# Logits of four units in one set of matmuls, the groups' work in small pieces between scans, and zeros written from SyncE's queue

## The chip, the cores and the metric

The kernel runs on one core of one Trainium2 chip. The time is the device time of one launch in microseconds (us); the time of the kernel before is the median of three runs.

## What is computed

The input is a batch of 4 sequences of 5056 tokens with 256 features (20224 tokens in all, fp32). A gated recurrence runs along each sequence; its output goes to a router that picks one of 8 experts for each token; each expert keeps the 80 tokens it weighs highest and runs a two-layer network on them. All other tokens get zeros.

```python
sig = 1.0 / (1.0 + np.exp(-f_logit))
f = lower_bound + (1.0 - lower_bound) * sig
for t in range(S):                       # S = 5056, for 4 sequences and 256 features
    h = f[:, t] * h + (1.0 - f[:, t]) * x[:, t]
    y[:, t] = h
logits = y.reshape(20224, 256) @ w_gate  # 8 experts
expert_idx = np.argmax(logits, axis=1)
gate_w = softmax(logits)[arange, expert_idx]
out = np.zeros((20224, 256))
for e in range(8):
    tok_idx = the 80 tokens of expert e with the largest gate_w
    h = np.maximum(x[tok_idx] @ w1[e], 0.0)          # 256 x 1024
    out[tok_idx] = gate_w[tok_idx, None] * (h @ w2[e])
```

## The kernel before, in words

**First stage.** The work is cut into 40 units of 512 tokens: 10 groups, each with one unit of each of the 4 sequences. A unit goes through SP (`load`: its tiles `f_t` and `x_t`, 512 KB each, 4 buffers each), ACT (`gate`: the sigmoid, in place), POOL (`enter`: the product, in place), PE (`to_channels`: 8 transposes of `f_t` into the PSUM tiles `sp`, 8 of `x_t` into `up`, so that features are on the partitions), ACT (`decay`: writes the factors into the unit's place in `h_all`) and DVE (`scan`: the recurrence, two scans of 512 steps, one for each half `o` of the features, in place in `h_all` with `up` as second operand). `h_all` is one large SBUF tile with the states of all 20224 tokens.

**The groups' work.** `logits` multiplies a unit's states with the router's weights on PE. The four interleaved token positions `r` go to four strips of 32 output partitions, so the moving operand is read with a step of 4 elements (16 bytes). The result of a group is the PSUM tile `lg`; ACT copies it to `ls`; PE transposes it back to tokens, `lt`; DVE finds the largest logit and its expert (`mx`, `shift`, `eq`, `pick`). After groups 3, 6, 8 and 9 a batch of further steps follows (exponentials on ACT, `sums`, `gated` with DVE and POOL, `turned` on PE, `candidates`, `peaks`), one job in each round of the main loop. The round `n` writes, in this order: load n+3, gate n+2, enter n+2, transposes n+1, decay n+1, scan n, logits n-1, then a group's `by_token` and `choice`, then one job. The order of instructions on each engine is the order in which the code writes them; an engine that waits holds up all that stands behind it.

**Selection.** From the largest candidates of each partition DVE and PE rank the tokens of all experts; `trow` holds the chosen token numbers. This is a single chain (lines 419 to 492).

**Experts.** For each expert the 80 states are copied out of `h_all` by DVE (28), ACT (28) and POOL (24), each of which first loads its token numbers from `trow` into its registers (line 515); `scaled` makes `xt`; then `hidden` (PE, `h_ps`), `relu` (ACT), `result` (PE, `y_ps`), `finish` (DVE) and `scatter` (POOL, rows of the output). The weights come over SP's queue into a ring of 7 tiles of 512 KB. All output rows are first written with zeros: 20 transfers of about 1 MB, which ACT issues before its first `gather`:

```python
    w_sb = {}
    for key in order[:3]:
        w_sb[key] = weights(*key)
    for k in clears:
        clear(nc.scalar, k)
```

PSUM has 8 banks: `sp` 2, `up` 3, `lg`, `lt` and `ct` (the turned candidates) 1 each.

Of the kernel before, what the change touches and what calls it, by code (L numbers as in the profile page):

```python
# [22 lines left out]
def kernel(  # L23
# [128 lines left out]
    with tc.tile_pool(name="ld", bufs=4) as ld, \  # L152
         tc.tile_pool(name="gsm", bufs=1) as gsm, \
         tc.tile_pool(name="pss", bufs=2, space=PSUM) as pss, \
         tc.tile_pool(name="psu", bufs=3, space=PSUM) as psu, \
         tc.tile_pool(name="plg", bufs=1, space=PSUM) as plg:

        xs, fs, sts, uts, sps, ups, lgs, lts, shs, gts, gms, cts = ({} for _ in range(12))
# [6 lines left out]
        def setup():  # L165
# [7 lines left out]
            bp = plg.tile([P, 1], F32, name="bp", tag="lt")  # L173
# [59 lines left out]
        def logits(n):  # L233
            g, b = divmod(n, B)
            if b == 0:
                lgs[g] = plg.tile([P, B, P], F32, name="lg", tag="lg")
            hv = h_all[:, :, ds(spot(n), G)].rearrange("c o (p r) -> c o p r", r=R)
            for o in range(DC):
                for r in range(R):
                    nc.tensor.matmul(lgs[g][ds(r * LC, LC), b], wg[:, o], hv[:, o, :, r],  # L240
                                     start=o == 0, stop=o == DC - 1, skip_group_check=True)

        def by_token(g):
            ls = gsm.tile([P, B, P], F32, name="ls", tag="ls")
            nc.scalar.copy(ls, lgs.pop(g))  # L245
            lt = plg.tile([P, B, P], F32, name="lt", tag="lt")
# [11 lines left out]
        def choice(g):  # L258
# [23 lines left out]
        def sums(g0, g1):  # L282
            n = g1 - g0
            sm = gsm.tile([P, per_batch, C], F32, name="sm", tag="sm")[:, ds(0, n)]
            nc.vector.tensor_reduce(sm, shs.pop(g0)[:, ds(0, n)], AX.X, ALU.add)
# [4 lines left out]
        def gated(g):  # L290
# [397 lines left out]
```

## Time and profile before

| | |
|---|---|
| median of three runs | 302.87 us (302.01 to 303.67) |
| the profiled execution, its own time | 303.26 us |
| its span in the trace | 301.4 us |
| busy in the span: PE, DVE, POOL, ACT | 207.6, 180.6, 135.2, 133.3 us |
| bytes read and written | 58.73 MB and 21.36 MB |
| mean granted TensorE clock | 0.848 of full speed |

A trace tells of one execution. Busy shares are averages over the three stages, which have different limits; what a stage waits for is read in the stage itself. In rows of the timeline, the two numbers at the front are the start and the length of a run of equal instructions in us, and in brackets stands the idle time of the engine ahead of it and what ended it. "x16" counts records: an fp32 matmul is two records, a transpose one.

### The profile page before, as it was taken

Reading aid. Unit: us, or ns where it says so; the run is one execution under the profiler, and the core shown is the slowest. Engines: PE = TensorE matmul, PEld = TensorE weight load, DVE = VectorE, ACT = ScalarE, POOL = GpSimd, SP = SyncE. Lnnn points to the kernel's source line nnn. Section 1 sums busy time; section 2 is a strip of 40 time slices with the busy share of each in tenths; the row PEclk is TensorE's granted clock in tenths of the full one; section 3 lists DMA queues with packets and bytes.
Section 4 is the critical chain, followed back from the end, with each engine's and each line's share of the span. In section 5 each row is a group of like instructions: output and inputs, shape, how many; then the busy total and the mean of one; then the engine's idle time right before and its main releaser. Section 6 shows DMA issues by size and latency. Waiting matters only on the chain.

```text
span 301.4 us, 5943 instructions
## 1 busy us (share of the span) xinstructions
PE 207.6 (69%) x1756; PEld 162.6 (54%) x1756; DVE 180.6 (60%) x484; ACT 133.3 (44%) x380; POOL 135.2 (45%) x269
## 2 busy tenths in 40 slices
PE   1798596979978896979797420610003999999991
PEld 1676375757655575657575100600003988888870
DVE  1996685858497969679596579314002715665500
ACT  3676456573796564786665100000005454555110
POOL 3876837465646784638581101003403405555111
PEclk9999899797999998998999955575555559999998
DMA  7999979596979896887920999999994448999900
GB/s 211 349 348 350 341 233 324 198 313 198 290 226 299 249 346 198 242 263 220 318 79 0 335 372 409 409 406 388 384 383 157 142 139 265 312 310 305 327 27 27
DMA packets 66439, 80.55 MB, mean 267 GB/s; under 512 B 2784, under 2 KB 52064, under 8 KB 66400
## 3 DMA queue, kind: packets, MB, share of 16 engines
q1 hardware_dynamic: 55040, 58.73, 61.4%
q10 hardware_dynamic: 10976, 20.72, 18.2%
q0 software_dynamic: 384, 0.66, 0.7%
q8 instruction: 16, 0.26, 0.4%
q14 instruction: 23, 0.19, 0.2%
HBM read 58.73 MB, written 21.36 MB: 266 GB/s over the span
## 4 chain that ended last, share of the span: by engine, by line
PE 56%; DVE 17%; issue 14%; ACT 5%; DMA 5%; POOL 1%; SPq 0%; POOLq 0%; DVEq 0%; ACTq 0%
PE lg L240 12%; PE h_ps L537 12%; PE y_ps L552 10%; PE sp L215 9%; PE up L215 8%; DVE h_all L228 6%; ACT h_all L222 3%; DVE eq L271 3%; DMA f_t<-in_f_logit_dram 3%; DVE beat L449 3%; PE lt L248 2%; DMA x_t<-in_x_dram 2%; ACT ls L245 2%; PE flat_p L472 1%; DVE mx L268 1%
## 5 line engine op out<-in xcount | busy, mean ns | idle before, releaser
L209 POOL TENSOR_TENSOR x_t<-f_t,x_t 128x1024 f32<-128x1024 f32 x40 | 94.9, 2375 | 50.2 <-ACT f_t L205 33.6
L228 DVE TENSOR_TENSOR_SCAN h_all<-h_all,up 128x512 f32<-128x512 f32 x80 | 96.2, 1253 | 6.2 <-PE up L215 5.2
L222 ACT ACTIVATE h_all<-sp,nomlb 128x512 f32<-128x512 f32 x80 | 51.1, 684 | 50.4 <-PE sp L215 50.3
L215 PE MATMUL up<-ident,x_t 128*128 128x128 f32 x320 | 48.3, 293 | 22.2 <-DVE h_all L228 20.3
L537 PE MATMUL h_ps<-xt,w_sb 128*128 128x80 f32 x256 | 36.4, 311 | 33.5 <-issue 33.5
L537 PEld LDWEIGHTS h_ps<-xt,w_sb 128*128 128x128 f32 x256 | 36.1, 227 | 34.3 <-issue 33.8
L215 PEld LDWEIGHTS up<-ident,x_t 128*128 128x128 f32 x320 | 40.1, 153 | 25.5 <-issue 20.9
L519 ACT COPY xe<-h_all 128x2 f32 x224 | 22.2, 190 | 67.3 <-DMA out_dram<-zero 56.0
L215 PE MATMUL sp<-ident,f_t 128*128 128x128 f32 x320 | 48.2, 299 | 3.4 <-ACT f_t L205 3.4
L240 PE MATMUL lg<-h_all,wg 128*32 128x128 f32 x640 | 43.9, 404 | 5.4 <-ACT ls L245 4.8
L215 PEld LDWEIGHTS sp<-ident,f_t 128*128 128x128 f32 x320 | 39.7, 154 | 13.4 <-ACT f_t L205 7.0
L205 ACT ACTIVATE f_t<-f_t 128x1024 f32<-128x1024 f32 x40 | 42.4, 1059 | 8.8 <-DMA f_t<-in_f_logit_dram 8.8
L519 POOL COPY xe<-h_all 128x2 f32 x192 | 24.5, 202 | 39.2 <-DVE xt L526 18.5
L519 DVE COPY xe<-h_all 128x2 f32 x224 | 26.5, 180 | 19.6 <-issue 19.6
L552 PE MATMUL y_ps<-w_sb,hid 128*80 128x256 f32 x128 | 30.1, 391 | 0.0
L240 PEld LDWEIGHTS lg<-h_all,wg 128*32 128x32 f32 x640 | 18.3, 120 | 19.2 <-ACT ls L245 7.0
L552 PEld LDWEIGHTS y_ps<-w_sb,hid 128*80 128x80 f32 x128 | 19.4, 156 | 8.1 <-issue 1.0
L561 POOL DMA_INDIRECT out_dram<-y,goal x8 | 7.5, 940 | 34.9 <-DVE y L558 32.5
L268 DVE TENSOR_REDUCE mx<-lt 128x16 f32<-128x128 f32 (+1 forms) x10 | 2.9, 291 | 28.0 <-PE lt L248 28.0
L526 DVE TENSOR_SCALAR xt<-xe,omlb 128x80 f32<-128x80 f32 x16 | 3.5, 258 | 23.6 <-ACT xe L519 22.8
L545 ACT ACTIVATE hid<-h_ps 128x320 f32<-128x320 f32 x16 | 7.0, 436 | 20.8 <-PE h_ps L537 20.8
L558 DVE TENSOR_SCALAR y<-y_ps,gsl 80x256 f32<-80x256 f32 x8 | 3.8, 480 | 20.4 <-PE y_ps L552 20.4
(96 smaller groups left out, 107.2 us busy)
## 6 DMA issues: line engine op xcount, KB each, us to landing
f_t<-in_f_logit_dram SPq DMA_DIRECT2D x40, 512.0 KB, 4.7
x_t<-in_x_dram SPq DMA_DIRECT2D x40, 512.0 KB, 5.3
out_dram<-zero ACTq DMA_DIRECT2D x19, 1024.0 KB, 13.1
w_sb<-in_moe_w_dram SPq DMA_DIRECT2D x32, 512.0 KB, 4.7
out_dram<-zero ACTq DMA_DIRECT2D x1, 768.0 KB, 12.2
out_dram<-y,goal POOLq DMA_INDIRECT x8, 4.0
lb<-in_lower_bound_dram ACTq DMA_DIRECT2D x1, 1.0 KB, 4.1
wg<-in_moe_w_gate_dram ACTq DMA_DIRECT2D x1, 8.0 KB, 5.3
```

The costliest lines, as they stand in the source:

```text
L205: nc.scalar.activation(sts[n], sts[n], ACT.Sigmoid, scale=-1.0)
L209: nc.gpsimd.tensor_tensor(uts[n], sts[n], uts[n], ALU.mult)
L215: nc.tensor.transpose(ps[:, ds(r * P, P)], src[n][:, r, ds(o * P, P)], ident)
L222: nc.scalar.activation(h_all[:, o, ds(spot(n), G)], sps.pop((n, o)), ACT.Identity, scale=nomlb[:, ds(o, 1)], bias=1.0)
L228: nc.vector.tensor_tensor_scan(h, h, ups.pop((n, o)), h_all[:, o, ds(spot(n) - 1, 1)] if n >= B else 0.0, ALU.mult, ALU.add)
L240: nc.tensor.matmul(lgs[g][ds(r * LC, LC), b], wg[:, o], hv[:, o, :, r], start=o == 0, stop=o == DC - 1, skip_group_check=True)
L271: nc.vector.scalar_tensor_tensor(out=eq, in0=sh, scalar=0.0, in1=revexp[:n_p].unsqueeze(1).broadcast_to(full), op0=ALU.is_ge, op1=ALU.mult)
L449: nc.vector.tensor_scalar(beat, rivals, vals[:, ds(k, 1)], 0.0, ALU.is_gt, ALU.add, accum_out=rank[:, ds(k, 1)])
L519: copy(X[e][:, :, ds(k + j, 1)], h_all[:, :, ds(v, 1)])
L537: nc.tensor.matmul(h_ps[:, c], halves[i][:, o, ds(c * P, P)], xt[:, o], start=o == 0, stop=o == DC - 1, skip_group_check=True)
L552: nc.tensor.matmul(y_ps, hid[:, c], halves[c // CH][:, c % CH], start=c == 0, stop=c == FC - 1)
L561: nc.gpsimd.indirect_dma_start(out=out, out_offset=bass.IndirectOffsetOnAxis(ap=goal[:, ds(e, 1)], axis=0), in_=Y.pop(e), in_offset=None, ...
```

## The change

- `logits` takes a whole group at once: 8 matmuls with 512 moving columns instead of 32 with 128, written one round after the group's last scan was written; the copy to `ls` follows it directly in the code.
- The work of a group is three jobs, one in each round after the scan: `logits`; `by_token` with `mx` and `shift`; `eq` with `pick`. Of the batch's jobs, `sums` is cut in two. In the last two rounds two batch jobs run instead of one, and all that is left runs behind the loop.
- `lt` shares the bank of `lg`; `up` has 4 buffers instead of 3.
- The product `gm` of the last three groups is made by DVE instead of POOL.
- The zeros are issued by SP: 14 behind the first six weight tiles, the other 6 in the first expert's round, behind the weights of its successors.

```diff
-         tc.tile_pool(name="psu", bufs=3, space=PSUM) as psu, \
+         tc.tile_pool(name="psu", bufs=4, space=PSUM) as psu, \
...
-        def logits(n):
-            g, b = divmod(n, B)
-            if b == 0:
-                lgs[g] = plg.tile([P, B, P], F32, name="lg", tag="lg")
-            hv = h_all[:, :, ds(spot(n), G)].rearrange("c o (p r) -> c o p r", r=R)
+        def logits(g):
+            lg = plg.tile([P, B * P], F32, name="lg", tag="lg")
             for o in range(DC):
+                hv = h_all[:, o].rearrange("c (b s) -> c b s", b=B)[:, :, ds(first(g), G)]
+                hv = hv.rearrange("c b (p r) -> c b p r", r=R)
                 for r in range(R):
-                    nc.tensor.matmul(lgs[g][ds(r * LC, LC), b], wg[:, o], hv[:, o, :, r],
+                    nc.tensor.matmul(lg[ds(r * LC, LC)], wg[:, o], hv[:, :, :, r],
                                      start=o == 0, stop=o == DC - 1, skip_group_check=True)
+            lss[g] = gsm.tile([P, B, P], F32, name="ls", tag="ls")
+            nc.scalar.copy(lss[g].rearrange("p b t -> p (b t)"), lg)
...
-            nc.gpsimd.tensor_tensor(
+
+            (nc.gpsimd if g < n_grp - 3 else nc.vector).tensor_tensor(
...
-        n = -AHEAD
-        while n < n_unit + 3 or todo:
+        for n in range(-AHEAD, n_unit):
             unit(load, n + AHEAD)
...
             unit(scan, n)
-            unit(logits, n - 1)
-            group(by_token, n - 2)
-            group(choice, n - 2)
-            for job in todo[:1]:
-                for f in job:
-                    f()
-            del todo[:1]
-            group(lambda g: todo.extend(work(*batches[g])) if g in batches else None, n - 2)
-            n += 1
+            some_of(of_group, 1)
+            some_of(of_batch, 1 if n < n_unit - 2 else 2)
+            if n >= 0 and n % B == B - 1:
+                g = n // B
+                of_group += [[lambda g=g: logits(g)], [lambda g=g: shifted(g)],
+                             [lambda g=g: chosen(g)]]
...
-    for k in clears:
-        clear(nc.scalar, k)
+    zeros = list(clears)
+
+    def clear_some(m):
+        for k in zeros[:m]:
+            clear(nc.sync, k)
+        del zeros[:m]
+
+    clear_some(14)
...
                     more(1)
+                if e == 0 and not again:
+                    clear_some(len(zeros))
                 y_ps = result(e)
```

PE, at the end of a group in the kernel before (`sp` and `up` are transposes, `lg` the logits, `lt` the transposes back; in brackets the engines whose progress an instruction waits for):

```order
L215 MATMUL up<-ident,x_t 128x128 [waits DVE_49]
L215 MATMUL up<-ident,x_t 128x128 x3
L240 MATMUL lg<-h_all,wg 32x128 [waits PE_49,Activation_49]
L240 MATMUL lg<-h_all,wg 32x128 x7
L248 MATMUL lt<-ident,ls 128x128 x4
L215 MATMUL sp<-ident,f_t 128x128 [waits PE_49]
L215 MATMUL sp<-ident,f_t 128x128 x3
L215 MATMUL sp<-ident,f_t 128x128 [waits PE_49]
L215 MATMUL sp<-ident,f_t 128x128 x3
L215 MATMUL up<-ident,x_t 128x128 [waits DVE_49,Pool_49]
```

The same place on PE in the changed kernel:

```order
L239 MATMUL lg<-h_all,wg 32x512 [waits DVE_49,Activation_49]
L239 MATMUL lg<-h_all,wg 32x512 x3
L239 MATMUL lg<-h_all,wg 32x512 [waits DVE_49,Activation_49]
L239 MATMUL lg<-h_all,wg 32x512 x3
L215 MATMUL sp<-ident,f_t 128x128 [waits PE_49]
L215 MATMUL sp<-ident,f_t 128x128 x3
L215 MATMUL sp<-ident,f_t 128x128 [waits PE_49]
L215 MATMUL sp<-ident,f_t 128x128 x3
L215 MATMUL up<-ident,x_t 128x128 [waits Pool_49]
L215 MATMUL up<-ident,x_t 128x128 x7
L248 MATMUL lt<-ident,ls 128x128 [waits Activation_49]
L248 MATMUL lt<-ident,ls 128x128 x3
```

The transposes back stand a whole unit's transposes behind the logits now, and each half of the logits waits for DVE and for ACT.

DVE, in the first groups of the kernel before (the scans have the tile `h_all` as output):

```order
L228 SCALAR_TENSOR_TENSOR h_all<-h_all,up 128x512 [waits PE_49,Activation_49] x6
L268 TENSOR_REDUCE mx<-lt 128x16 [waits PE_49]
L269 TENSOR_TENSOR shift<-lt,mx 128x128 [waits DVE_49]
L271 SCALAR_TENSOR_TENSOR eq<-shift,revexp 128x128 [waits DVE_49]
L274 TENSOR_REDUCE pick<-eq 128x16 [waits DVE_49]
L228 SCALAR_TENSOR_TENSOR h_all<-h_all,up 128x512 [waits Activation_49] x2
```

The same place on DVE in the changed kernel:

```order
L228 SCALAR_TENSOR_TENSOR h_all<-h_all,up 128x512 [waits PE_49,Activation_49] x6
L269 TENSOR_REDUCE mx<-lt 128x16 [waits PE_49]
L270 TENSOR_TENSOR shift<-lt,mx 128x128 [waits DVE_49]
L228 SCALAR_TENSOR_TENSOR h_all<-h_all,up 128x512 [waits Activation_49] x2
L278 SCALAR_TENSOR_TENSOR eq<-shift,revexp 128x128 [waits DVE_49]
L281 TENSOR_REDUCE pick<-eq 128x16 [waits DVE_49]
```

The four steps that stood together are cut in two by the scans of one unit.

ACT's instructions at the end of the first stage of the kernel before (`shift` is the last exponential, `trow` the load of token numbers into registers, `xe` the first of 28 copies):

```order
L280 ACTIVATE shift<-shift 128x128
L147 DMA out_dram<-zero 128x4x512 x19
L147 DMA out_dram<-zero 128x3x512
L515 TENSOR_LOAD trow
L519 ISA
L519 COPY xe<-h_all 128x2
```

All 20 issues stand between the last exponential and the first register load; in the changed kernel ACT has none of them. SP's queue in the changed kernel, behind the last loads (`w_sb` are the weight tiles):

```order
L408 DMA w_sb<-in_moe_w_dram 128x2x512 x4
L412 DMA w_sb<-in_moe_w_dram 128x4x256 x2
L147 DMA out_dram<-zero 128x4x512 x14
L408 DMA w_sb<-in_moe_w_dram 128x2x512 x2
L412 DMA w_sb<-in_moe_w_dram 128x4x256 x2
L147 DMA out_dram<-zero 128x4x512 x5
L147 DMA out_dram<-zero 128x3x512
L408 DMA w_sb<-in_moe_w_dram 128x2x512 x2
```

On SP the zeros stand in two runs, 14 and 6, each ahead of weight tiles.

## Rows read from the trace of the kernel before

**Rows 1.** Busy time by stage; then TensorE clock, DMA share, GB/s.

```profile
core 0: us, PE busy (x) PEld busy (x) DVE busy (x) ACT busy (x) POOL busy (x), PEclk, DMA share, GB/s
22.70:167.70 145.00, 119.05 (x1207) 88.35 (x1205) 111.16 (x132) 89.97 (x122) 85.36 (x43) 0.94 0.79 247
167.70:196.70 29.00, 8.95 (x53) 6.52 (x53) 18.74 (x69) 0.90 (x2) 2.95 (x9) 0.59 1.04 389
196.70:230.70 34.00, 0.25 (x2) 0.18 (x2) 4.86 (x41) 2.74 (x28) 6.11 (x48) 0.54 0.99 371
```

**Rows 2.** The chain that ended last, from selection to experts.

```profile
196.48 0.23 DVE trow L474
...
197.14 33.52 issue
230.66 7.09 PE h_ps L537 x32
...
237.87 7.04 PE h_ps L537 x32
244.91 4.68 PE y_ps L552 x16
...
253.12 3.46 PE y_ps L552 x16
```

**Rows 3.** Timeline of ACT from the last logits to its first expert copies.

```profile
168.54 0.59 ACT L245 COPY ls<-lg 128x512 f32<-128x512 f32 x1 [3.99 <-PE lg L240]
...
171.22 49.03 ACTq L147 DMA_DIRECT2D out_dram<-zero  x20
227.46 2.74 ACT L519 COPY xe<-h_all 128x2 f32 x28 [55.96 <-DMA out_dram<-zero]
```

**Rows 4.** Timeline of DVE: the copies of the first and the fourth expert.

```profile
205.82 2.80 DVE L519 COPY xe<-h_all 128x2 f32 x24 [0.26 <-issue]
...
251.68 3.26 DVE L519 COPY xe<-h_all 128x2 f32 x28 [1.57 <-issue]
```

**Rows 5.** DVE by line, 13 to 168 us: busy, mean ns; idle before, releasers.

```profile
L228 DVE TENSOR_TENSOR_SCAN h_all<-h_all,up 128x512 f32<-128x512 f32 x80 | 96.2, 1253 | 6.2 <-PE up L215 5.2 <-ACT h_all L222 1.0
L271 DVE SCALAR_TENSOR_TENSOR eq<-shift,revexp 128x128 f32<-128x128 f32 (+1 forms) x9 | 8.5, 939 | 0.4
...
L268 DVE TENSOR_REDUCE mx<-lt 128x16 f32<-128x128 f32 (+1 forms) x9 | 2.6, 291 | 26.9 <-PE lt L248 26.9
```

**Rows 6.** Timeline of ACT: two sigmoids that waited for their loads.

```profile
17.43 1.06 ACT L205 ACTIVATE f_t<-f_t 128x1024 f32<-128x1024 f32 x1 [0.32 <-DMA f_t<-in_f_logit_dram]
...
20.45 1.06 ACT L205 ACTIVATE f_t<-f_t 128x1024 f32<-128x1024 f32 x1 [0.30 <-DMA f_t<-in_f_logit_dram]
```

**Rows 7.** Timeline of DVE behind the last scan.

```profile
167.64 0.40 DVE L285 TENSOR_REDUCE sm<-shift 128x32 f32<-128x256 f32 x1
...
177.05 0.26 DVE L419 MAX8 vals<-tops 128x8 f32<-128x96 f32 x1
```

**Rows 8.** The zeros' transfers (KB, us to landing), and SP's first weight tiles.

```profile
out_dram<-zero ACTq DMA_DIRECT2D x19, 1024.0 KB, 13.1
...
164.81 1.90 SPq L386 DMA_DIRECT2D w_sb<-in_moe_w_dram  x4
```

**Rows 9.** The register loads (line 515): shortest, median and longest in ns.

```profile
L515 DVEq TENSOR_LOAD <-trow x8: 1849/1858/7112, 197.7 to 277.6; - x8
```

**Rows 10.** Timeline of PE at full clock.

```profile
85.62 1.10 PE L240 MATMUL lg<-h_all,wg 128*32 128x128 f32 x16
86.66 1.09 PE L215 MATMUL sp<-ident,f_t 128*128 128x128 f32 x8
87.58 1.04 PE L215 MATMUL up<-ident,x_t 128*128 128x128 f32 x8
```

**Rows 11.** Timeline of PE at half clock, and the clock of that stretch.

```profile
52.95 1.12 PE L240 MATMUL lg<-h_all,wg 128*32 128x128 f32 x16
54.00 1.97 PE L215 MATMUL sp<-ident,f_t 128*128 128x128 f32 x8
...
52.80:56.00 3.20, 3.20 (x28) 2.55 (x27) 2.87 (x3) 0.69 (x1) 1.17 (x1) 0.50 0.46 156
```

More of the change, by code (lines that the diff above doesn't have):

```diff
@@ L154 @@
          tc.tile_pool(name="pss", bufs=2, space=PSUM) as pss, \
-         tc.tile_pool(name="psu", bufs=3, space=PSUM) as psu, \
+         tc.tile_pool(name="psu", bufs=4, space=PSUM) as psu, \
          tc.tile_pool(name="plg", bufs=1, space=PSUM) as plg:
-        xs, fs, sts, uts, sps, ups, lgs, lts, shs, gts, gms, cts = ({} for _ in range(12))
+        xs, fs, sts, uts, sps, ups, lss, lts, shs, gts, gms, cts, sms = ({} for _ in range(13))
         def spot(n):
@@ L172, in setup @@
                            channel_multiplier=0, allow_small_or_imprecise_dtypes=True)
-            bp = plg.tile([P, 1], F32, name="bp", tag="lt")
+            bp = plg.tile([P, 1], F32, name="bp", tag="lg")
             nc.tensor.transpose(bp, base_row, ident[:1, :1])
@@ L230, in scan @@
                     h_all[:, o, ds(spot(n) - 1, 1)] if n >= B else 0.0, ALU.mult, ALU.add)
-        def logits(n):
-            g, b = divmod(n, B)
-            if b == 0:
-                lgs[g] = plg.tile([P, B, P], F32, name="lg", tag="lg")
-            hv = h_all[:, :, ds(spot(n), G)].rearrange("c o (p r) -> c o p r", r=R)
+        def logits(g):
+            lg = plg.tile([P, B * P], F32, name="lg", tag="lg")
             for o in range(DC):
+                hv = h_all[:, o].rearrange("c (b s) -> c b s", b=B)[:, :, ds(first(g), G)]
+                hv = hv.rearrange("c b (p r) -> c b p r", r=R)
                 for r in range(R):
-                    nc.tensor.matmul(lgs[g][ds(r * LC, LC), b], wg[:, o], hv[:, o, :, r],
+                    nc.tensor.matmul(lg[ds(r * LC, LC)], wg[:, o], hv[:, :, :, r],
                                      start=o == 0, stop=o == DC - 1, skip_group_check=True)
+            lss[g] = gsm.tile([P, B, P], F32, name="ls", tag="ls")
+            nc.scalar.copy(lss[g].rearrange("p b t -> p (b t)"), lg)
         def by_token(g):
-            ls = gsm.tile([P, B, P], F32, name="ls", tag="ls")
-            nc.scalar.copy(ls, lgs.pop(g))
-            lt = plg.tile([P, B, P], F32, name="lt", tag="lt")
+            ls = lss.pop(g)
+            lt = plg.tile([P, B, P], F32, name="lt", tag="lg")
             for b in range(B):
@@ L255, in begin, with shifted @@
             return batch_of(g)[0]
-        def choice(g):
+        def shifted(g):
+            by_token(g)
             n_p = rows(g)
@@ L269, in choice @@
             nc.vector.tensor_tensor(sh, lg, mx.unsqueeze(2).broadcast_to(full), ALU.subtract)
+        def choice(g):
+            n_p = rows(g)
+            full = [n_p, C, E]
+            sh = shs[begin(g)][:n_p, g - begin(g)]
             eq = gsm.tile([P, C, E], F32, name="eq", tag="eq")[:n_p]
@@ L283, in sums, with inverses @@
             n = g1 - g0
-            sm = gsm.tile([P, per_batch, C], F32, name="sm", tag="sm")[:, ds(0, n)]
-            nc.vector.tensor_reduce(sm, shs.pop(g0)[:, ds(0, n)], AX.X, ALU.add)
+            sms[g0] = gsm.tile([P, per_batch, C], F32, name="sm", tag="sm")
+            nc.vector.tensor_reduce(sms[g0][:, ds(0, n)], shs.pop(g0)[:, ds(0, n)], AX.X, ALU.add)
+        def inverses(g0, g1):
+            n = g1 - g0
+            sm = sms.pop(g0)[:, ds(0, n)]
             nc.vector.tensor_scalar_add(sm, sm, 1e-9)
@@ L322, in work @@
         def work(g0, g1):
-            jobs = [[lambda: exponentials(g0, g1)], [lambda: sums(g0, g1)]]
+            jobs = [[lambda: exponentials(g0, g1)], [lambda: sums(g0, g1)],
+                    [lambda: inverses(g0, g1)]]
             for g in range(g0, g1 + 1):
@@ L335, in unit, with chosen, some_of @@
                 f(m)
-        def group(f, m):
-            if 0 <= m < n_unit and m % B == B - 1:
-                f(m // B)
         AHEAD = 3
-        todo = []
+        of_group, of_batch = [], []
+        def chosen(g):
+            choice(g)
+            if g in batches:
+                of_batch.extend(work(*batches[g]))
+        def some_of(jobs, k):
+            while jobs and k:
+                for f in jobs.pop(0):
+                    f()
+                k -= 1
         setup()
-        n = -AHEAD
-        while n < n_unit + 3 or todo:
+        for n in range(-AHEAD, n_unit):
             unit(load, n + AHEAD)
```

4 lines of the change are left out of this document (added).

## The prediction

> **What bounds the kernel now.** I read the stages first [rows 1]. In the first stage (to 167.7 us) no engine is full: DVE is busy 111 of 145 us, PE 119, and DMA moves 247 GB/s. Selection (to 196.7) and the wait behind it (to 230.7) have DMA at 371 to 389 GB/s, its share at 1.0: there the zeros set what DMA does. From 196.7 to 230.7 no engine computes for long.
>
> The chain of waits says what that last stretch is [rows 2]: the chosen tokens (`trow`) are ready at 196.71, and the first expert's matmuls start at 230.66, 33.9 us later. ACT explains it [rows 3]: its 20 zero issues begin at 171.22 and hold its queue for 49.0 us, so that its 28 copies for the first expert run from 227.46 to 230.20. DVE had its own copies done at 205.82 + 2.80 = 208.62 [rows 4]. So ACT's queue alone is late, by 21.6 us.
>
> In the first stage the view by line shows what DVE, the busiest engine in order, waits for [rows 5]: 26.9 us for `lt` (nine times, 3.0 us each) and 6.2 us ahead of scans. DMA isn't the limit there: where sigmoids wait for loads they follow each other by 3.02 us [rows 6], 12.1 us for a group, and a group takes some 16 (144.9 us from the fifth unit's scan at about 22.7 to the last scan's end at 167.64 [rows 1, 7], for nine groups).
>
> **The change part by part.**
>
> *Zeros off ACT.* ACT can load its token numbers when `trow` is there. DMA stays full at that time: six weight tiles (3.1 MB) and 14 zero transfers (14.7 MB) take 46 us at 389 GB/s [rows 1], from about 4 us ahead of the last scan's end (SP issues the tiles when the last `up` is done, now at 164.81 [rows 8]). `trow` comes some 28 us behind that end. A register load took 7.1 us under the zeros and 1.85 us otherwise [rows 9]. I keep 7.1: the first matmul then starts at 208.62 + 0.46 (what now lies between ACT's last copy and it) = 209.1 where it stood at 230.66. **-21.6 us.** With a fast load it would be 5.3 more, with ACT's load starting late up to 2 less.
>
> *The logits of four units.* Sixteen records of 128 columns take 1.04 us to the next stage's start, at 0.23 for four strips that run together [rows 10]. At half clock the same sixteen take as long, 1.12 against 1.10, while eight transposes go from 1.09 to 1.97 [rows 10, 11]. So the clock doesn't set the strips' pace. A contiguous transpose of 128 columns takes 0.115 (eight in 0.92), half of 0.23: I take the read with its step of 16 bytes as the limit, which grows with the columns. Four strips of 512 columns then cost 0.9 us, a half of the features 1.8, a group 3.6 (four times 1.04 now). Bounds: 1.8 us a group if long strips run at the contiguous pace, 7.4 if all sixteen records run one after the other.
>
> By the Trainium skill, SBUF — State Buffer, section "Door 1: The DMA port swizzle", accesses hit full bandwidth when at least two fall in one 16-byte line. A step of four fp32 values puts one in each, which agrees with the factor of two above. The skill's TensorEngine Tiling (Array Packing), section "Tiling Modes", says that tiles run independently, which by itself would give the 1.8 us; the first of the rivals is that case.
>
> *What the logits hold up.* They read all four sequences' places in `h_all` at once. The reordered rows of PE show that this read is taken as the whole stretch between: each half of `lg` waits for DVE and ACT anew, and the `up` behind it no longer waits for DVE. So it waits for the scan of the unit after the group (u0) and the decay of the next (u1), and u1's scans wait for it. With u0's first scan starting at 0 and 1.2 us for a scan [rows 5]: first half of `lg` 1.25 to 3.25 (with 0.2 of drain), u1's first scan at 3.3 where it could at 2.4; second half to 5.05, u1's second scan at 5.1 where it could at 4.5. **DVE waits 1.45 us in each of nine groups, +13.** Behind `lg` stand 16 transposes (0.9 us for eight [rows 10]), to 6.75, and then `lt`, to 7.4; `ls` (0.59 [rows 3]) fits beside them. DVE ends u1's scans at 6.3 and waits 1.1 us for `lt`: **nine times, +10, where it was 26.9.** `eq`, delayed to 0.94 us by POOL's work, stays [rows 5]. Of the scans' own 6.2 us I take off 2.5, since PE stands still for shorter and falls less to half clock (bounds 0 and 6.2). Sum of the first stage: -26.9 + 13 + 10 - 2.5 = **-6.5 us**. The fourth `up` buffer and the shared bank of `lt` cost nothing in this: `lt` needs `ls`, which empties the bank; were that cover gone, the next logits would wait, but they come 8 us later.
>
> *The tail.* From the last scan to `vals` it is 9.4 us now [rows 7]. The leftovers of groups 7 and 8 run under the last logits and DVE makes `gm` without POOL; the last half of logits is 1.1 us longer. I take 8.0, **-1.4** (bounds -2.5 and +1).
>
> *The six late zeros.* SP reaches them when the first half of the second expert's `h_ps` has freed its tile, 10.7 us behind the first matmul [rows 2]. They are 6.0 MB, 15.5 us at 389 GB/s, to 26. The first `y_ps` ends at 18.9 (244.91 + 4.68 - 230.66). DVE then loads the numbers of the fourth expert; now its copies end at 254.94 [rows 4], and the matmuls that need them start at 256.58 (253.12 + 3.46 [rows 2]). With 0.5 for `xt` that leaves 1.1 us, and a load of 7.1 instead of 1.85 takes 5.25: PE stands for 4.2 us. The weights of that expert, behind the zeros in the queue, come at about 28 where 25.9 would do, inside the same stall. The next expert's load meets the weights' backlog, 1.8 more: **+6 us** (bounds 0 and 10, the latter with a fall to half clock).
>
> Sum: -21.6 - 6.5 - 1.4 + 6 = -23.5. The profiled execution took 303.26, so 279.8; it lies 0.4 above the median of the runs, which makes 279.4. **I predict 280 us.**
>
> **The rivals.**
>
> *Long strips run at the contiguous pace* (1.8 us a group). Then u1's scans hardly wait: first half done at 2.4, second at 3.5. Nine times 1.5 us less, about 266. For it speaks that the four start together; against it the same pace at both clocks. Chance 0.16.
>
> *The second stall is worse, or groups stay near 15.5 us*, because the exponentials hold ACT and with it the decay that `lg` now waits for: 288 to 297. For it speaks that each group's pieces now wait on each other in order; against it ACT's 90 busy us in 145 [rows 1]. Chance 0.10.
>
> *Slower than before: the sixteen long records run one after the other*, 7.4 us a group. u1's second scan moves by the whole difference: 3.8 us nine times, 34, which gives 314. It decides from 6.2 us a group on (3.6 + 23.5 / 9). Against it: sixteen records of 128 columns in 1.04 us is less than the 1.84 of a single file. Chance 0.03.
>
> *No gain*: the zeros' issue holds SP as it held ACT, and the tile that SP then has to bring is wanted at once. For it speaks that three of its weight tiles stand behind 14 zeros; against it that the first six tiles stand ahead, and are enough to 18.9 us behind the first matmul. 302, chance 0.01.
>
> **How the numbers follow.** My forecast has 0.70 (272 to 288, by the bounds of its terms). 264 to 291 holds it, the contiguous case and about half of the worse one, over 0.8. No change within 0.5% (what a measurement here can tell) 0.01, slower 0.03, faster 0.96.
>
> **What the profile after would show.** ACT's idle time ahead of its first `xe` without `zero` as releaser, and the first `h_ps` about 12.4 us behind `trow`. DVE's wait for `lt` near 10 us in all; scans that wait for `lg`, about 13 us. Sixteen `lg` records in about 3.8 us. The last scan's end near 161. Long register loads in the first and the fourth expert, and an idle PE of some 4 us ahead of the fourth `h_ps`. Wrong I would be if four strips of 512 columns took far from 0.9 us, or if the register loads were slow for another reason than the zeros.

## The result, and the profile after

The changed kernel takes 292.67 us (median of four runs, 291.17 to 293.64) where the kernel before, run beside it, took 303.27: a ratio of 0.9652 (95% interval 0.96 to 0.9705). The forecast was 280, with a range of 264 to 291. The sign was right; the time lies 1.7 us above the range and 12.7 above the forecast.

The profiled execution took 292.59 us, with a span of 290.8 us, 10.6 shorter than before. The stages first, cut at the last scan's end, at `trow` and at the first expert's matmul (columns as in [rows 1]):

```profile
22.70:165.30 142.60, 114.78 (x758) 71.58 (x756) 116.79 (x134) 87.41 (x122) 84.94 (x43) 0.95 0.80 254
165.30:193.40 28.10, 10.65 (x58) 6.61 (x53) 19.96 (x72) 0.90 (x2) 1.70 (x6) 0.62 1.03 388
193.40:205.70 12.30, 0.21 (x1) 0.11 (x1) 4.73 (x40) 2.74 (x28) 3.02 (x24) 0.64 1.05 399
```

The wait behind `trow` is 12.3 us long where it was 34. But the first stage is only 2.4 us shorter (its last scan ends at 165.3, before at 167.7), and DVE works longer in it: 116.8 us against 111.2 [rows 1]. What comes behind the wait is on PE's timeline:

```profile
205.74 7.09 PE L565 MATMUL h_ps<-xt,w_sb 128*128 128x80 f32 x32 [11.96 <-issue]
...
214.10 7.12 PE L565 MATMUL h_ps<-xt,w_sb 128*128 128x80 f32 x32 [1.15 <-DVE xt L554]
221.01 5.13 PE L580 MATMUL y_ps<-w_sb,hid 128*80 128x256 f32 x16
225.98 3.69 PE L565 MATMUL h_ps<-xt,w_sb 128*128 128x80 f32 x32
229.51 3.62 PE L580 MATMUL y_ps<-w_sb,hid 128*80 128x256 f32 x16
240.91 7.09 PE L565 MATMUL h_ps<-xt,w_sb 128*128 128x80 f32 x32 [7.78 <-DMA w_sb<-in_moe_w_dram]
```

The fourth expert's `h_ps` starts after 7.78 us of idle PE, waiting for weights, and then takes 7.09 us where the third took 3.69. The same place in the chain of waits, and SP's queue (a row is the start of the first issue and the time until the last is through):

```profile
228.15 12.63 DMA w_sb<-in_moe_w_dram
240.91 7.09 PE h_ps L565 x32
248.00 5.18 PE y_ps L580 x16
253.18 3.53 PE h_ps L565 x32
```

```profile
212.86 5.34 SPq L412 DMA_DIRECT2D w_sb<-in_moe_w_dram  x2
218.25 9.80 SPq L147 DMA_DIRECT2D out_dram<-zero  x6
228.15 3.10 SPq L408 DMA_DIRECT2D w_sb<-in_moe_w_dram  x2
```

The weights were issued as soon as the six zeros were through SP, and still took 12.63 us to land; a tile of weights takes 5.2 in the median. Three stretches of this time (the columns again as in [rows 1]) show a full DMA, an idle PE, and the clock behind it:

```profile
220.00:232.00 12.00, 12.00 (x66) 9.54 (x66) 0.51 (x2) 3.83 (x31) 1.06 (x9) 0.83 1.05 398
234.00:238.00 4.00, 0.00 (x0) 0.00 (x0) 3.30 (x25) 0.35 (x3) 0.00 (x0) 0.96 0.96 291
242.00:250.00 8.00, 8.00 (x35) 7.15 (x35) 1.42 (x11) 0.88 (x3) 4.12 (x26) 0.50 0.97 325
```

PE stands still to 240.9 and then runs at 0.50, that is at 1.2 GHz, to 250 at least. The copies of the fourth expert on DVE's timeline:

```profile
233.01 3.26 DVE L547 COPY xe<-h_all 128x2 f32 x28 [6.35 <-issue]
236.41 0.43 DVE L554 TENSOR_SCALAR xt<-xe,omlb 128x80 f32<-128x80 f32 x2
```

DVE waited 6.35 us there for its register load (before 1.57, [rows 4]): with the weights in time PE would have stood from 233.1 to 236.8.

In the first stage, DVE by line (13 to 168 us, as [rows 5]) has the new waits as forecast, 12.4 us for `lg` and 8.9 for `lt`:

```profile
L228 DVE TENSOR_TENSOR_SCAN h_all<-h_all,up 128x512 f32<-128x512 f32 x80 | 97.6, 1258 | 14.3 <-PE lg L239 12.4 <-issue 1.0 <-ACT h_all L222 0.8
...
L269 DVE TENSOR_REDUCE mx<-lt 128x16 f32<-128x128 f32 (+1 forms) x9 | 2.6, 291 | 8.9 <-PE lt L248 8.9
```

But some of its small steps are long: `eq` takes 1.04 us in the mean, 0.94 before [rows 5]. A single one shows why. DVE's and POOL's timelines at 75 to 88 us:

```profile
75.52 2.44 DVE L228 TENSOR_TENSOR_SCAN h_all<-h_all,up 128x512 f32<-128x512 f32 x2
77.88 1.31 DVE L278 SCALAR_TENSOR_TENSOR eq<-shift,revexp 128x128 f32<-128x128 f32 x1
79.23 0.29 DVE L281 TENSOR_REDUCE pick<-eq 128x16 f32<-128x128 f32 x1
...
85.21 1.82 DVE L297 TENSOR_SCALAR sm<-sm 128x64 f32<-128x64 f32 x1
```

```profile
74.36 4.68 POOL L209 TENSOR_TENSOR x_t<-f_t,x_t 128x1024 f32<-128x1024 f32 x2 [4.97 <-ACT f_t L205]
82.31 4.67 POOL L209 TENSOR_TENSOR x_t<-f_t,x_t 128x1024 f32<-128x1024 f32 x2 [3.26 <-ACT f_t L205]
```

POOL's two products run back to back from 74.36 to 79.04; `eq` starts inside and ends at 79.19, just behind them. `sm` starts at 85.21 and ends at 87.03, behind the second pair's end at 86.98. `pick`, which starts at 79.23, takes 0.29. So some DVE steps are held until POOL's product is through, whatever their own length. The Trainium skill, SBUF — State Buffer, section "SBUF: two separate sides", says that DVE and GpSimd (POOL) share a pair of ports which an instruction holds for its whole length, and that this concerns DVE operations in a two-port mode or with two SBUF inputs. These ends agree with it, and e10 below tries the operand.

### The profile page after: what moved, and what is told of

Read it like the earlier page. It is cut to its first block, busy times and chain, and to the rows that moved or that the text cites. A ratio compares the mean times of both kernels' runs of the same rounds, so it can differ in the third digit from the quotient of the medians.

```text
span 290.8 us, 4980 instructions
## 1 busy us (share of the span) xinstructions
PE 207.8 (71%) x1276; PEld 148.4 (51%) x1276; DVE 187.6 (65%) x487; ACT 130.6 (45%) x380; POOL 133.0 (46%) x266
## 4 chain that ended last, share of the span: by engine, by line
PE 33%; DMA 17%; DVE 16%; issue 16%; POOL 11%; DVEq 3%; ACT 2%; SPq 1%; POOLq 0%; ACTq 0%
POOL x_t L209 11%; PE h_ps L565 10%; PE y_ps L580 9%; DMA x_t<-in_x_dram 9%; DMA w_sb<-in_moe_w_dram 8%; DVE h_all L228 7%; PE up L215 5%; PE lg L239 4%; DVE beat L477 3%; DVEq L543 2%; PE sp L215 2%; PE flat_p L500 2%; DVE xe L547 1%; DVE oh L306 1%; DVE at L462 1%
## 5 line engine op out<-in xcount | busy, mean ns | idle before, releaser
L209 POOL TENSOR_TENSOR x_t<-f_t,x_t 128x1024 f32<-128x1024 f32 x40 | 94.2, 2370 | 56.7 <-ACT f_t L205 48.1
L228 DVE TENSOR_TENSOR_SCAN h_all<-h_all,up 128x512 f32<-128x512 f32 x80 | 97.6, 1258 | 14.3 <-PE lg L239 12.4
L565 PE MATMUL h_ps<-xt,w_sb 128*128 128x80 f32 x256 | 39.8, 330 | 20.9 <-issue 12.0
L215 PE MATMUL sp<-ident,f_t 128*128 128x128 f32 x320 | 46.1, 287 | 8.8 <-ACT h_all L222 5.2
L215 PEld LDWEIGHTS up<-ident,x_t 128*128 128x128 f32 x320 | 36.8, 147 | 27.7 <-POOL x_t L209 22.9
L565 PEld LDWEIGHTS h_ps<-xt,w_sb 128*128 128x128 f32 x256 | 39.4, 244 | 21.9 <-issue 20.2
L215 PEld LDWEIGHTS sp<-ident,f_t 128*128 128x128 f32 x320 | 37.1, 147 | 24.8 <-issue 12.5
L239 PE MATMUL lg<-h_all,wg 128*32 128x512 f32 x160 | 38.0, 1078 | 6.7 <-DVE h_all L228 6.6
L580 PE MATMUL y_ps<-w_sb,hid 128*80 128x256 f32 x128 | 32.1, 410 | 0.0
L242 ACT COPY ls<-lg 128x512 f32<-128x512 f32 x10 | 5.9, 586 | 50.5 <-PE lg L239 50.5
L580 PEld LDWEIGHTS y_ps<-w_sb,hid 128*80 128x80 f32 x128 | 20.5, 165 | 9.1 <-issue 2.5
L573 ACT ACTIVATE hid<-h_ps 128x320 f32<-128x320 f32 x16 | 6.9, 435 | 23.1 <-PE h_ps L565 22.7
L239 PEld LDWEIGHTS lg<-h_all,wg 128*32 128x32 f32 x160 | 5.0, 118 | 23.7 <-issue 18.6
L278 DVE SCALAR_TENSOR_TENSOR eq<-shift,revexp 128x128 f32<-128x128 f32 (+1 forms) x10 | 9.6, 964 | 0.0
## 6 DMA issues: line engine op xcount, KB each, us to landing
out_dram<-zero SPq DMA_DIRECT2D x19, 1024.0 KB, 13.3
```

What stands on the lines that cost most here:

```text
L209: nc.gpsimd.tensor_tensor(uts[n], sts[n], uts[n], ALU.mult)
L215: nc.tensor.transpose(ps[:, ds(r * P, P)], src[n][:, r, ds(o * P, P)], ident)
L228: nc.vector.tensor_tensor_scan(h, h, ups.pop((n, o)), h_all[:, o, ds(spot(n) - 1, 1)] if n >= B else 0.0, ALU.mult, ALU.add)
L239: nc.tensor.matmul(lg[ds(r * LC, LC)], wg[:, o], hv[:, :, :, r], start=o == 0, stop=o == DC - 1, skip_group_check=True)
L278: nc.vector.scalar_tensor_tensor(out=eq, in0=sh, scalar=0.0, in1=revexp[:n_p].unsqueeze(1).broadcast_to(full), op0=ALU.is_ge, op1=ALU.mult)
L565: nc.tensor.matmul(h_ps[:, c], halves[i][:, o, ds(c * P, P)], xt[:, o], start=o == 0, stop=o == DC - 1, skip_group_check=True)
```

## The experiments

Each kernel is the changed one with the edit shown, e2 the kernel before with an edit. Medians in us, ratios to the kernel before run on the same chip:

| run | median | ratio | 95% interval |
|---|---|---|---|
| changed kernel | 292.67 | 0.9652 | 0.96 to 0.9705 |
| e1 zeros on ACT again | 300.70 | 0.989 | 0.9857 to 0.9922 |
| e2 before, zeros moved | 295.52 | 0.9741 | 0.9678 to 0.9803 |
| e3 all zeros at once | 283.93 | 0.9345 | 0.9292 to 0.9398 |
| e4 `ls` behind the next sigmoid | 283.20 | 0.9315 | 0.9254 to 0.9375 |
| e5 setup early | 292.48 | 0.9639 | 0.9598 to 0.968 |
| e6 six zeros in the first stage | 279.37 | 0.9217 | 0.917 to 0.9263 |
| e7 logits unit by unit | 289.57 | 0.955 | 0.9509 to 0.9592 |
| e8 e4, e5, e6 together | 271.20 | 0.8942 | 0.8903 to 0.8982 |
| e9 e7 and a round between | 279.49 | 0.9203 | 0.9144 to 0.9262 |
| e10 one operand in PSUM | 290.03 | 0.9523 | 0.9446 to 0.96 |
| e11 e4, e6, e9, e10 together | 269.55 | 0.888 | 0.8824 to 0.8936 |
| e12 e11 without e10 | 267.23 | 0.8821 | 0.8755 to 0.8886 |

**e1 and e2: the two halves of the change apart.**

```diff
-            clear(nc.sync, k)
+            clear(nc.scalar, k)
...
-    clear_some(14)
+    clear_some(len(zeros))
...
-                if e == 0 and not again:
-                    clear_some(len(zeros))
```

> The changed kernel with the zeros issued by ACT again, where they stood before. It times the logits, the small pieces and the tail alone. Theory A (the first stage gave only what the trace of the changed kernel shows: last scan 2.4 us earlier, tail 1.2 shorter): 3.6 us under the kernel before, about 299.7 against 303.3, ratio 0.988. Rival B (the first stage gave the 7.9 us of the prediction and the zeros in SP's queue cost some of it): about 295.4, ratio 0.974. Either way ACT's copies of the first expert should again start some 55 us behind its last exponential.

For e2 the `clear_some` of the change went into the kernel before, 14 behind the first weights and the rest in the first expert's round.

> The kernel before with nothing but the zeros moved to SP, 14 and 6 as in the change. Theory A (the late six cost what the trace of the changed kernel shows, 14.3 us between the first matmul of the experts and the end): 303.3 - 21.6 + 14.3 = 296, ratio 0.976, with an idle PE of some 8 us ahead of the fourth expert's h_ps that ends with its weights, and PE at half clock behind it. Rival B (the late six cost the 6 us of the prediction, and the rest came from the earlier start of the experts stage in the changed kernel): 287.7, ratio 0.949.

e1 took 300.70, e2 295.52: theory A in both, within 1 us. In e1 ACT's copies stand behind the zeros again, 53.49 us after its last exponential. e2 has the first `h_ps` at 208.99, where the prediction had put it (209.1), and the same stall as the changed kernel:

```profile
208.99 7.09 PE L543 MATMUL h_ps<-xt,w_sb 128*128 128x80 f32 x32 [11.93 <-issue]
...
244.21 7.09 PE L543 MATMUL h_ps<-xt,w_sb 128*128 128x80 f32 x32 [8.06 <-DMA w_sb<-in_moe_w_dram]
```

So the logits and pieces alone are worth 3.3 us, the zeros' move alone 8.5, and together the change gave 10.6: the halves nearly add up, and each gave less than forecast.

**e3 and e6: the six late zeros elsewhere.** e3 issues all 20 at once (`clear_some(len(zeros))` for `clear_some(14)`, without the late call). e6 issues six in the first stage:

```diff
             unit(load, n + AHEAD)
+            clear_some(1 if n in (12, 16, 20, 24, 28, 32) else 0)
...
-    clear_some(14)
+    clear_some(len(zeros))
...
-                if e == 0 and not again:
-                    clear_some(len(zeros))
```

> The changed kernel with all 20 zeros behind the first six weight tiles, none late. Theory A (what costs is where the six stand: ahead of the weights of the fourth expert, with SP idle in between from 200 to 218 us and DMA below half its rate from 210 to 218): the zeros are through at about 222 us, the weights of the third expert come at about 225 where 226 would do, no register load behind 222 is long, the stall ahead of the fourth h_ps and the half clock behind it are gone: 292.7 - 13 = about 280, ratio to the kernel before 0.923. Rival B (the bytes cost the same wherever they stand): the stall moves to the third expert's weights, with half clock behind it, 289 to 293.

> The changed kernel with the six late zeros issued by SP in the first stage, one behind the loads of every fourth unit from the round of unit 12 on, and the other 14 where they are. Theory A (the late burst costs the 8 us stall ahead of the fourth h_ps and the 5.3 us of half clock behind it, and the first stage has room: DMA moved 261 GB/s in 80 to 115 us where 383 to 409 were seen under the zeros): 292.7 - 13 = about 279.5, ratio to the kernel before 0.922, no idle PE over 1.5 us between the second h_ps and the end, last scan as before within 1 us. Rival B (loads that stand behind 1 MB of zeros come late, and DVE, which sets the pace, waits for them): last scan 5 to 15 us later, 284 to 294, with sigmoids that wait for loads.

e3 gained 8.7 us, between the theories. The stall went from the fourth to the third expert and is shorter; DVE's register loads of the second and third expert took 6.6 us (the profiled execution took 287.55 us):

```profile
230.23 5.87 PE L565 MATMUL h_ps<-xt,w_sb 128*128 128x80 f32 x32 [2.49 <-DMA w_sb<-in_moe_w_dram]
```

e6 took 279.37, theory A's 279.5. Its first `h_ps` starts at 206.38, and from there the span (277.2) has 70.8 us to run; before it was 70.7 (301.4 less 230.66), in the changed kernel 85.1. The first stage paid 0.5 us at most: the last scan ends at 165.8 instead of 165.3, with DMA at 318 GB/s instead of 261 in 80 to 115 us. The fourth `h_ps` follows without a wait, and the clock stays at 1.00:

```profile
232.24 3.69 PE L565 MATMUL h_ps<-xt,w_sb 128*128 128x80 f32 x32
```

```profile
242.00:250.00 8.00, 8.00 (x59) 6.92 (x58) 5.00 (x38) 3.77 (x31) 4.96 (x34) 1.00 0.95 319
```

So where the six stand costs the changed kernel 13.3 us, with the half clock in it.

**e4: ACT's copy of the logits.**

```diff
-            lss[g] = gsm.tile([P, B, P], F32, name="ls", tag="ls")
-            nc.scalar.copy(lss[g].rearrange("p b t -> p (b t)"), lg)
+            lgs[g] = lg
+
+        def emptied():
+            for g in list(lgs):
+                lss[g] = gsm.tile([P, B, P], F32, name="ls", tag="ls")
+                nc.scalar.copy(lss[g].rearrange("p b t -> p (b t)"), lgs.pop(g))
...
             unit(gate, n + 2)
+            emptied()
```

`shifted` calls `emptied` too, for what is left behind the loop.

> The changed kernel with the copy of lg to ls written one round later on ACT, behind the next sigmoid and ahead of the next decay; nothing else moves. Theory A (ACT, held by the copy for up to 6 us in each group, delays the next sigmoid, with it POOL's product, the transposes and the decay, and that is what kept the first stage long): groups get shorter by 0.3 to 0.5 us, the last scan ends 3 to 4 us earlier, about 289.5, ratio to the kernel before 0.954. Rival B (u1's scans wait for the logits whatever ACT does, and the sigmoid comes early enough): 292.7, ratio 0.965, with POOL's waits for ACT gone but the scans' waits for lg as they were.

It gained 9.5 us, more than theory A had. The path was another: DVE's waits for `lg` (12.7) and `lt` (8.8) stayed, POOL's for ACT fell from 48.1 to 22.5. What went is much of the holding: up to the last scan's end `eq` takes 5.4 us in all instead of 9.3 and `oh` 3.2 instead of 4.3, and 1.9 us that `shift` waited for the step of POOL that clears it are gone. That is 6.9 us, and the last scan ends 6.6 us earlier, at 158.7. The same group as above, DVE and then POOL:

```profile
77.03 0.27 DVE L284 SCALAR_TENSOR_TENSOR eq<-shift,revexp 128x128 f32<-128x128 f32 x1
```

```profile
74.68 2.37 POOL L210 TENSOR_TENSOR x_t<-f_t,x_t 128x1024 f32<-128x1024 f32 x1 [3.61 <-ACT f_t L206]
```

With the sigmoid ahead of the copy, POOL's product stands alone here and not in a pair, and at 77.05 it is through: 0.27 us instead of 1.31. From the u1 scan that waits for `lg` to the next group's it took 14.36 us (56.59 to 70.95), here 13.31 (56.79 to 70.10): the difference is that of one `eq`. (The profiled execution took 285.31 us; its span is 7.4 us shorter than that of the changed kernel, and 6.7 of them are there at `trow`.)

**e5: the steps ahead of the first scan.** Two setup steps on DVE are also held, and the first scan starts at 15.5 us where it started at 13.1 before. The edit moves the setup steps that need no load to the front of `setup`.

> The changed kernel with DVE's ten setup steps on row and column numbers written ahead of the two that wait for the loaded constants, so that they run before POOL's first product (7.25 us); nothing else moves. Theory A (a DVE step that starts during a POOL product is held until the product ends; in the changed kernel two of these steps, 2.33 and 2.46 us instead of 0.28, put the first scan 2.5 us later than in the kernel before, and no later group gives that back since DVE sets the pace): the steps take 0.3 us or less, the first scan starts at 13.1 us or earlier, the last scan ends 2.3 us earlier: 290.4, ratio to the kernel before 0.957. Rival B (the loads set the pace up to 42 us, so the late start is absorbed there): 292.7, ratio 0.965.

292.48: rival B. The steps took 0.3 us or less (the two that now stand behind them were held instead, 2.51 us against 0.39), and the first scan started at 10.8, but the second group's u1 scan started where it did, at 27.75 (27.90 in the changed kernel, 25.65 before). Its waits in e5 and in the kernel before, on DVE's timelines (in the changed kernel it is 1.03 us):

```profile
27.75 1.28 DVE L229 TENSOR_TENSOR_SCAN h_all<-h_all,up 128x512 f32<-128x512 f32 x1 [2.92 <-issue]
```

```profile
25.65 2.45 DVE L228 TENSOR_TENSOR_SCAN h_all<-h_all,up 128x512 f32<-128x512 f32 x2 [0.47 <-ACT h_all L222]
```

In this stretch the loads set the pace, and the logits come right ahead of that scan (PE starts the sixteen at 25.79): 2.25 us are lost there however early DVE begins. In e9, where the scan does not wait for the logits, it starts at 25.45.

**e7 and e9: the read of four places.**

```diff
-            for o in range(DC):
-                hv = h_all[:, o].rearrange("c (b s) -> c b s", b=B)[:, :, ds(first(g), G)]
...
+            for b in range(B):
+                hv = h_all[:, :, ds(spot(g * B + b), G)].rearrange("c o (p r) -> c o p r", r=R)
+                for o in range(DC):
+                    for r in range(R):
+                        nc.tensor.matmul(lg[ds(r * LC, LC), ds(b * P, P)], wg[:, o],
+                                         hv[:, o, :, r], start=o == 0, stop=o == DC - 1,
+                                         skip_group_check=True)
```

> The changed kernel with the logits as 32 matmuls of 128 columns, one sequence's place of h_all at a time, at the same place in the order. Theory A (the read of four places at once is taken as the whole stretch between them, so the logits wait for u0's scan and u1's decay and u1's scans wait for them: 12.4 us of DVE's waits): these waits go, the sixteen long records of 3.8 us become 64 short ones of 4.3, the wait for lt stays within 0.5 us a group: last scan 8 to 11 us earlier, 282 to 285, ratio to the kernel before about 0.934. Rival B (the long matmuls as such are what scans wait for, since PE is as full as DVE): the waits for lg turn into waits for up, 291 to 295.

```profile
L228 DVE TENSOR_TENSOR_SCAN h_all<-h_all,up 128x512 f32<-128x512 f32 x80 | 95.9, 1252 | 2.1 <-PE lg L239 1.3 <-ACT h_all L222 0.8
L270 DVE TENSOR_REDUCE mx<-lt 128x16 f32<-128x128 f32 (+1 forms) x9 | 2.6, 292 | 20.5 <-PE lt L249 20.5
```

The waits for `lg` went as theory A said, 12.4 to 1.3 us, though the 64 short records of a group take 3.89 us where the sixteen long ones took 3.79, and those for `lt` rose from 8.9 to 20.5: 289.57, neither theory's time. DVE only stands one step later. e9 adds an empty job between `logits` and `shifted`:

> The changed kernel with the logits unit by unit as in e7 and one empty job between the logits and the step that turns them back (so by_token with mx and shift stands two rounds behind the logits instead of one). Theory A (in e7 DVE's waits for lg, 12.4 us, came back as waits for lt, 20.5 instead of 8.9, only because mx stands one round behind; with a round between, DVE runs two more scans first): the waits for lt fall under 6 us, those for lg stay under 2, the last scan ends some 12 to 15 us before that of e7 (163.0), where the loads' pace of 12.1 us a group stops it: 274 to 278, ratio to the kernel before about 0.91. Rival B (PE has 12.2 us of work in a group and ACT is held by the ls copy, so scans wait for up and for their factors instead): 283 to 288.

```profile
L228 DVE TENSOR_TENSOR_SCAN h_all<-h_all,up 128x512 f32<-128x512 f32 x80 | 96.7, 1257 | 16.8 <-ACT h_all L222 15.9 <-PE lg L239 0.7
...
L270 DVE TENSOR_REDUCE mx<-lt 128x16 f32<-128x128 f32 (+1 forms) x10 | 2.9, 292 | 9.0 <-PE lt L249 9.0
```

279.49, 10.1 us better than e7 but short of theory A's 274 to 278: the waits for `lt` fell to 9.0, scans now wait 15.9 us for their factors from ACT, as rival B had it, and `eq` is held less (0.40 us).

**e10: what holds a DVE step.**

```diff
-         tc.tile_pool(name="psu", bufs=4, space=PSUM) as psu, \
+         tc.tile_pool(name="psu", bufs=3, space=PSUM) as psu, \
...
+        rv = plg.tile([P, E], F32, name="rv", tag="rv")
+        nc.vector.tensor_copy(rv, revexp)
...
-                out=eq, in0=sh, scalar=0.0, in1=revexp[:n_p].unsqueeze(1).broadcast_to(full),
+                out=eq, in0=sh, scalar=0.0, in1=rv[:n_p].unsqueeze(1).broadcast_to(full),
```

`oh` reads `rv` as well.

> The changed kernel with the small constant that eq and oh read (revexp) held in PSUM instead of SBUF; for its bank up has 3 buffers instead of 4. Theory A (a DVE step with both inputs in SBUF is held while a POOL product runs, one with an input in PSUM, as shift, is not: 0.29 us always): eq falls from 1.04 to 0.3 us, oh from 0.54 to 0.3, waits for lg and lt stay at 21 us in all, the last scan ends 6 to 9 us earlier: 284 to 287, ratio to the kernel before about 0.941. Rival B (any DVE step is slowed beside POOL, or the third up buffer is missed): 291 to 295.

By line (13 to 168 us), the group shown above on DVE and on POOL, and the stretch from the second group's u1 scan to the tenth's (columns as in [rows 1]):

```profile
L278 DVE SCALAR_TENSOR_TENSOR eq<-shift,rv 128x128 f32<-128x128 f32 (+1 forms) x10 | 2.6, 264 | 0.0
```

```profile
78.59 0.26 DVE L278 SCALAR_TENSOR_TENSOR eq<-shift,rv 128x128 f32<-128x128 f32 x1
```

```profile
75.07 4.69 POOL L209 TENSOR_TENSOR x_t<-f_t,x_t 128x1024 f32<-128x1024 f32 x2 [4.43 <-ACT f_t L205]
```

```profile
30.23:151.93 121.70, 103.67 (x682) 64.00 (x678) 93.82 (x114) 79.43 (x110) 78.00 (x40) 0.97 0.85 272
```

On the mechanism theory A is right: with one input in PSUM `eq` takes 0.264 us in the mean and `oh` 0.271, though POOL's products run as before; the `eq` shown starts and ends inside one of them. `sm`, which the edit leaves alone, still takes 1.82 us. The time is 290.03, 2.6 us less than the changed kernel's, between the two theories and nearer to rival B. The stretch takes 121.70 us where the changed kernel takes 126.33: DVE is busy for 9.4 us less in it, and 4.8 of these come back as waits. And the group in the DMA-bound start is 2.3 us later (the u1 scan at 30.23 instead of 27.90, DMA at 324 instead of 349 GB/s in 13 to 45 us), which I put down to the missing `up` buffer; nothing else of the edit touches that stretch.

**e8, e11, e12: together.** e8 is e4, e5 and e6 in one kernel. e11 is e4, e6, e9 and e10, e12 the same without e10.

> The changed kernel with the ls copy behind the next sigmoid, the setup steps ahead of POOL's first product and the six zeros in the first stage. Theory A (the three costs lie on the path one behind the other and are of different places): 292.7 - 9.5 - 2.3 - 13 = about 268, ratio to the kernel before 0.884. Rival B (with a first stage of some 142 us the loads and 6 MB of zeros, 47 MB, need 335 GB/s, near the 349 GB/s of its DMA-bound start, so the loads take the pace over): 272 to 278.

> The changed kernel with the ls copy behind the next sigmoid, six zeros in the first stage, logits unit by unit with a round between, and the constant in PSUM. Theory A (DVE's waits and held steps are gone, and the loads set the pace: 41.4 MB and 6.3 MB of zeros at the 349 GB/s of the DMA-bound start are 137 us from 5 us on, so the last scan ends at 145 to 150; from it to the first h_ps 40.5 us as in the changed kernel, from there to the end 71): 257 to 263, ratio to the kernel before about 0.857. Rival B (the gains overlap, since each shortened the same wait of DVE): 265 to 271, about e8's time.

> The kernel of e11 with the constant back in SBUF and up with 4 buffers again. Theory A (in e11 scans waited 13.9 us for up, since the third buffer comes free late, and this costs more than held steps, which e9 without the constant in PSUM had at 0.40 and 0.36 us): waits for up fall under 4 us, 264 to 268. Rival B (the loads set the pace of the first stage in either, 349 to 369 GB/s up to 115 us, and both edits hide in it): 268 to 271, not to be told from e11.

e8 took 271.20, 3 us over theory A and just under rival B's range. DMA moves 350 GB/s in 45 to 80 us there: the loads begin to set the pace. e11 took 269.55 (rival B), e12 267.23, the fastest of all. Its median lies in theory A's range, but the waits for `up` fell only from 13.9 to 8.1 us, and the intervals of e11 and e12 overlap: what the `up` buffer is worth there is not settled. In e12 DMA is full to 115 us (354 GB/s in 45 to 80 us, 370 in 80 to 115), and `eq` takes 1.07 us again in the mean, at no visible cost.

## Why the prediction was right and wrong

The steps of the trace add up as follows: zeros off ACT -21.6, last scan -2.4, tail -1.2, selection +0.3, from the first `h_ps` to the end +14.3 (85.1 less 70.7); in all -10.6, the difference of the two spans. The prediction had -21.6, -6.5, -1.4, 0 and +6.

The time lies in the range of the rival that the prediction called "The second stall is worse, or groups stay near 15.5 us" (288 to 297, chance 0.10), and both of its halves came true: the stall was 7.8 us, and a group took 15.8 (126.33 us for eight, below). Its reason for the groups, that ACT holds the decay, is not what the trace shows: scans waited 0.8 us in all for ACT, and PE stood before `lg` 10.8 us for scans and 0.8 for ACT.

**Zeros off ACT: right.** The first `h_ps` starts 12.4 us behind `trow`, as forecast, with the slow register loads as forecast. e2 shows the term alone.

**The cost of the long logits: right.** Sixteen records take 3.79 us (3.6 to 3.8 had been worked out from the 16-byte step), DVE waits 12.4 us for `lg` (forecast 13) and 8.9 for `lt` (10). The rivals of the contiguous and of the serial pace are out. In e7 the waits for `lg` go when the read no longer spans four places, so they are the price of the read's extent and not of the time that the matmuls take. (In the prediction's sum, two times 0.9 us for the transposes end at 6.85 and not at 6.75; that moves the wait for `lt` by 0.1 us a group at most.)

**The sum of the first stage: wrong, by 4.1 us.** The step that failed is "`eq`, delayed to 0.94 us by POOL's work, stays". Between the second group's u1 scan and the tenth's, DVE's idle time fell from 30.5 to 23.1 us, by 7.4, even more than forecast; but its busy time rose by 3.4. The stretch before and after:

```profile
25.65:155.97 130.32, 107.05 (x1071) 80.22 (x1072) 99.80 (x115) 81.98 (x112) 80.92 (x41) 0.93 0.84 263
```

```profile
27.90:154.23 126.33, 103.02 (x682) 65.11 (x678) 103.21 (x115) 79.45 (x110) 78.36 (x40) 0.96 0.83 265
```

There are 115 instructions of DVE in both. By line in the same two stretches, before and after:

```profile
L271 DVE SCALAR_TENSOR_TENSOR eq<-shift,revexp 128x128 f32<-128x128 f32 x8 | 8.2, 1020 | 0.4
L295 DVE TENSOR_TENSOR oh<-revexp,pick 128x128 f32<-128x128 f32 x7 | 3.2, 463 | 0.0
...
L286 DVE TENSOR_SCALAR sm<-sm 128x64 f32<-128x64 f32 (+1 forms) x2 | 2.2, 1124 | 0.1
```

```profile
L278 DVE SCALAR_TENSOR_TENSOR eq<-shift,revexp 128x128 f32<-128x128 f32 x8 | 9.1, 1135 | 0.0
L306 DVE TENSOR_TENSOR oh<-revexp,pick 128x128 f32<-128x128 f32 x7 | 4.3, 614 | 0.0
L297 DVE TENSOR_SCALAR sm<-sm 128x64 f32<-128x64 f32 (+1 forms) x2 | 3.6, 1824 | 0.0
```

`eq` has 0.9 us of the 3.4, `oh` 1.1 and `sm` 1.4; for these two the prediction had no term at all. The pieces had been moved between scans, where more of their time falls into a product. That this holding is a matter of place, e4 shows, and what it hangs on for `eq` and `oh`, e10: without it the same stretch is 4.6 us shorter, even with one `up` buffer less. Another 2.25 us went at the start: in the stretch where the loads set the pace, the second group's u1 scan waits for the logits and the kernel before had nothing to give back there. Behind the tenth group's u1 scan 0.7 us were gained, so that -7.4, +3.4, +2.25 and -0.7 make the -2.4. The prediction charged each group 1.45 and set it against the old waits for `lt`, as if DVE set the pace from the first group on; e5 and e9 place these 2.25 us.

**The tail: right**, 8.2 us from the last scan to `vals` (165.24 to 173.46) where 8.0 was forecast.

**The six late zeros: mis-sized, +14.3 where +6 was forecast (bounds 0 and 10).** The place and the first mechanism are there: with DVE's load at 6.35 us PE would have stood for 3.7 us, forecast 4.2. What failed is "the weights of that expert ... come at about 28 ... inside the same stall". They came 35.0 us behind the first matmul (240.78), so the stall is 7.8. SP reached the zeros 12.5 us behind the first matmul, not 10.7, and from there to the landing it took 22.5 us, not 17: my sum counted 6.0 MB of zeros alone, where a weight tile just ahead and the two tiles themselves make 7.6 MB (estimated at the 398 GB/s of 220 to 232 us: 19 us), and the next weights shared the queue. Then came what had been kept only as a bound: behind the idle PE the clock is at 0.50, and `h_ps` and `y_ps` of that turn take 7.09 and 5.18 us instead of 3.53 and 3.46, 5.3 more. The rest is the second `h_ps`, 1.1 us late on its register load, since the 14 zeros still ran. 7.8 + 5.3 + 1.1 = 14.2. e6 takes the six away from there and gets 13.3 us back; that the stall brings the lower clock fits e2 and e3 (idle for 8.06 and 2.49 us, and a longer `h_ps` behind it) and e6 (neither), but was not tried by itself.

What stays open: why a register load takes 6 to 7 us while the zeros are written, and 1.85 otherwise. No run here changed that alone. Nor did a run bring the weights by another queue, so it is not shown whether their place behind the zeros held them, or only that DMA was full.

## What to carry to other kernels

When small steps are moved between the steps of the bounding engine, look at what the engine that can hold them (here POOL) does at the new place: a 0.3 us step took as long as the other engine's instruction had left, and an order that moves that engine's work (e4) can be worth more than the waits that one set out to remove. A burst of writes ahead of reads in one queue cost the reads their whole backlog here, their own bytes included, and as the wait idled PE, the slower clock behind it as well; the same writes spread over a stage whose DMA had room cost 0.5 us at most (e6). Removing a wait on the bounding engine is worth only what the next wait in its order leaves (e7), and the same goes for making its steps shorter (e10).

## What was not expected of the hardware

DVE steps with two SBUF inputs were held to the end of a running POOL product (`eq` 1.31 us instead of 0.29 in the case shown), and not at all with one input in PSUM (0.264 us). `sm`, with a single SBUF input, was held too (1.82 us, to 0.05 us behind the product); the Trainium skill, SBUF — State Buffer, section "SBUF: two separate sides", counts two-port modes among what is held, and no run here tried `sm` in another form. An idle time of PE of 7.8 us was followed by at least 8 us (242 to 250) at 1.2 GHz, while e6, without the stall, stayed at 2.4 in the same 8 us. And the register loads were long not only for the first expert: before its second set of copies POOL waited 6.18 us and ACT 6.36, while the last of the 14 zeros were still being written.
